# First expert of a routed two-layer kernel: when its weights are split, when the next choice begins, and how far ahead a count is placed

## The chip, the core and the metric

One core of a Trainium2 chip runs the whole kernel. The metric is the time on the device in microseconds, the median of three runs. TensorE (PE) multiplies, VectorE (DVE), ScalarE (ACT) and GpSimd (POOL) work element by element, and SyncE (SP) only issues transfers. Each engine carries out its own list of instructions in the order in which it was written; ACT and POOL issue transfers too, from the same list.

## The reference

Three stages follow one another. Attention with a causal mask and a bias gives x (2304 tokens of 512). Then a routed layer, then a dense one, each token by itself:

```python
logits = x @ w_gate                      # 8 experts, cap = 2304 // 8 = 288
for idx in np.argsort(-flat):            # greedy: best (token, expert) pairs first
    if assigned[tok] >= 0 or counts[e] >= cap: continue
    assigned[tok] = e; counts[e] += 1
out[mask] = np.maximum(x[mask] @ w1[e], 0.0) @ w2[e]     # w1 512x1024, w2 1024x512
...
h = x @ w_in                             # 512 x 2048
g = h * np.tanh(log1p(exp(h)))
return g @ w_out                         # 2048 x 512
```

## The kernel before, in words

All products keep float32 accuracy: each operand is split into a high part, rounded, and a low part, the rest, and a product is three matrix instructions (`mm3`, lines 447 to 449: high by high, high by low, low by high).

After attention, `experts` (line 181 on) fills the experts one after the other, the first one that is full first. `route(e)` finds on the chip which expert is filled next and with which 288 tokens. It takes the best logit of each token, then searches for the largest number of tokens by six counts: two of 64 bins, four of 32. Each count (`search`, line 252) writes a table of comparisons on DVE (`mask`, line 255), counts with 18 small matrix instructions (line 259, result in `rt`), makes `flags` on DVE (line 261), sums them with one more matrix instruction (line 263), and reads the result on DVE (line 267). Then it picks the expert (`ei`, line 315), numbers the tokens, gets their row numbers `idx` (lines 355 and 371) and has POOL gather the rows from memory, three transfers `xg` (line 376). `route` is a generator: each `yield n` says how many places (calls of `step`) of other work are written before its next piece. For the first expert there is no other work, and `route(0)` runs by itself in the loop at line 631. For the others it is written between the matrix products of the expert ahead; it begins at the place `side["next"]` (line 645: 48 places into the first expert, 4 into the later ones). Each group of twelve matrix instructions holds four places.

`up(e)` computes relu(x @ w1) @ w2 for the 288 tokens in eight blocks m of 128 hidden columns. Block m is one group of twelve instructions into a bank `hp` or `words`; ACT makes the high part of the activation (line 508) and DVE the low part (line 509); one group later the twelve instructions of the second layer follow for the block before, into `y`. Each group takes one piece of weights. Such a piece is loaded by SP (`raw`, line 408, 256 KB, four buffers), split by ACT (line 416, high part) and POOL (line 417, low part) into `wt`, which has four buffers. `feed` (line 420) writes loads and splits as buffers allow; `use` (line 431) calls it before a group takes its piece. At the end ACT and DVE turn `y` into `xu` (lines 526 and 527), and `down(e)` runs the dense layer with sixteen blocks f.

The dense layer's weights arrive as 64-bit words. `Convert` (line 32) turns them into floats once, early and beside the first expert: a transfer `r` issued by ACT (line 75, up to 512 KB, three buffers), three pieces on DVE (lines 112, 115, 118), a split by ACT (line 88) and POOL (line 89) into `WI` and `WO`. One call of `conv` writes one piece of DVE; three calls make a unit. `tick` writes one such call, four times for each block m of `up`. Since ACT holds its list while a transfer waits for its buffer, the order of lines 75, 88, 416 and 508 on ACT sets what waits for what. The last piece ahead of the first expert is `conv(5)` (line 640); then 50 idle products keep TensorE busy (`awake`, line 629), and `make_xt` transposes the gathered rows with 20 idle products after each of the three.

Of the kernel before, what the change touches and what calls it, by code (L numbers as in the profile page):

```python
# [28 lines left out]
def fb(ap):  # L29
    return ap.bitcast(F32)  # L30
# [169 lines left out]
def experts(ctx, tc, K, ring, ident, L, x_dram, w1, w2, cv, out):  # L200
# [22 lines left out]
    R = {}  # L223
# [9 lines left out]
    def hbank():  # L233
        if cv.done == 4 * NF2 and len(free) == 2:
            free.insert(0, words)
        free.append(free.pop(0))
        return free[-1]

    def inbank(name):
        at, n = place[name]  # L240
        return bank[:, at:at + n]


    def small(shape, dt, name, bufs=2):
        return rot.tile(shape, dt, name=name, bufs=bufs)

    def route(e):
# [5 lines left out]
        def search(T, lead):  # L253
            mask = small([128, NT, 64], F32R, "mask", 1)
            nc.vector.tensor_tensor(mask[:, :, :T], v[:, :, None].to_broadcast([128, NT, T]),  # L255
                                    jj[:, None, :T].to_broadcast([128, NT, T]), op=OP.is_ge)
            yield lead
            for c in range(NT):
                nc.tensor.matmul(bank[:E, :T], oh[:, c, :], mask[:, c, :T], start=c == 0, stop=c == NT - 1)  # L259
            yield 2  # L260
            nc.vector.tensor_scalar(flags[:E, :T], bank[:E, :T], CAP - 0.5, None, op0=OP.is_ge)
            yield 3
            nc.tensor.matmul(bank[:, 64:64 + T], onesF, flags[:, :T], start=True, stop=True)
            yield 2
            fl = small([128, 64], BF16, "fl", 1)
            J = small([128, 1], F32, "J")
            nc.vector.tensor_scalar(fl[:, 1:T], bank[:, 65:64 + T], 0.5, None, op0=OP.is_ge, op1=OP.add,
                                    accum_out=J)
            R["J"] = J

        if e == E - 1:
            ge = v
            nc.vector.tensor_scalar(ge, m, NEG / 16, None, op0=OP.is_ge)
        else:
            sign = small([128, NT], I32, "sign", 1)
            nc.vector.tensor_scalar(sign, m.bitcast(I32), 31, 0x7FFFFFFF, op0=OP.arith_shift_right,
                                    op1=OP.bitwise_and)
            key, low, high = inbank("sr").bitcast(I32), inbank("low"), inbank("high")
            nc.vector.tensor_tensor(key, m.bitcast(I32), sign, op=OP.bitwise_xor)
            nc.vector.tensor_scalar(high.bitcast(I32), key, 20, 0x4B000800, op0=OP.logical_shift_right,  # L280
                                    op1=OP.bitwise_xor)
            nc.vector.tensor_scalar(v, high, -float(2 ** 23), 2.0 ** -6, op0=OP.add, op1=OP.mult)
            first = search(64, 8)
            n = next(first)
            nc.vector.tensor_scalar(low.bitcast(I32), key, 0xFFFFF, 0x4B000000, op0=OP.bitwise_and,
                                    op1=OP.bitwise_or)
            lf = small([128, NT], F32, "lf", 1)
            nc.vector.tensor_scalar(lf, low, -float(2 ** 23), 2.0 ** -15, op0=OP.add, op1=OP.mult)
            yield n
            yield from first  # L290
            nc.vector.tensor_scalar(v, v, R["J"], 64.0, op0=OP.subtract, op1=OP.mult)
            yield from search(64, 8)
            nc.vector.tensor_scalar(v, v, R["J"], -1.0, op0=OP.subtract, op1=OP.max)
            nc.vector.tensor_scalar(v, v, 1.0, 32.0, op0=OP.min, op1=OP.mult)
            nc.vector.tensor_tensor(v, v, lf, op=OP.add)
            for i in range(4):
                yield from search(32, 6)
                nc.vector.tensor_scalar(v, v, R["J"], 32.0 if i < 3 else 1.0, op0=OP.subtract, op1=OP.mult)
            ge = m
            nc.vector.tensor_scalar(ge, v, 0.0, None, op0=OP.is_ge)  # L300
# [13 lines left out]
        ei = small([1, 1], I32, "ei")  # L314
# [36 lines left out]
        at = bank if e else spare  # L351
# [14 lines left out]
        idx = small([128, NJ], I32, "idx", 3)  # L366
# [26 lines left out]
    raw, wt = {}, {}  # L393
    at = {"load": 0, "split": 0, "use": 0}
    NRAW, NWT = 4, 4

    def load():
        e, m, k = seq[at["load"]]
        at["load"] += 1
        if m == 0 and k == 1:  # L400
            R[e, "reg"] = nc.sync.value_load(R[e, "ei"][0:1, 0:1], min_val=0, max_val=E - 1)
        ev = R[e, "reg"]
        t = rot.tile([128, NC, 128], F32, name="raw", bufs=NRAW)
        if k == 1:
            src = w1[ds(ev, 1), :, 128 * m:128 * m + 128].rearrange("o (c p) f -> p (o c) f", p=128)
        else:
            src = w2[ds(ev, 1), 128 * m:128 * m + 128, :].rearrange("o p (c f) -> p (o c) f", c=NC)
        nc.sync.dma_start(out=t, in_=src)
        raw[e, m, k] = t

    def split():
        key = seq[at["split"]]
        at["split"] += 1
        r = raw.pop(key)
        t = rot.tile([128, 2, NC, 128], F32R, name="wt", bufs=NWT)
        nc.scalar.activation(t[:, 0], r, AF.Copy)  # L416
        nc.gpsimd.tensor_sub(t[:, 1], r, fb(t)[:, 0])  # L417
        wt[key] = t

    def feed(most=99):  # L420
        while True:
            n = at["load"]
            if n < len(seq) and n < at["split"] + NRAW and (seq[n][0], "ei") in R:
                load()
            elif most and at["split"] < min(at["use"] + NWT, at["load"]):
                split()
                most -= 1
            else:
                return

    def use(key):
        assert seq[at["use"]] == key
        feed()
        at["use"] += 1
        return wt.pop(key)

    def conv(n):
        for _ in range(n):
            next(cv.steps, None)
# [13 lines left out]
    side = {"route": None, "at": 0, "next": 0, "conv": (1, 1)}  # L453
# [4 lines left out]
    def tick():  # L458
        now[0] += 1
        for fn, args in todo.pop(now[0], []):  # L460
            fn(*args)
        conv(side["conv"][now[0] % 2])
# [26 lines left out]
    def hl(t):  # L489
        return t[:, 0], t[:, 1]  # L490
# [3 lines left out]
    def up(e):  # L494
        xt = XT.pop(e)
        y, hs = [], {}
        for m in range(NF1 + 1):
            if m < NF1:
                t1 = use((e, m, 1))
                p = hbank()  # L500
                for c in range(NC):
                    mm3(p[:, :CAP], (t1[:, 0, c], t1[:, 1, c]), (xt[:, 0, c], xt[:, 1, c]), c == 0, c == NC - 1)
                    if c < NC - 1:
                        step()
                    if c == 1:
                        tick()
                h = ring("act", [128, 2, CAP], F32R)
                nc.scalar.activation(h[:, 0], p[:, :CAP], AF.Relu)  # L508
                nc.vector.scalar_tensor_tensor(h[:, 1], p[:, :CAP], 0.0, fb(h)[:, 0], op0=OP.max, op1=OP.subtract)
                hs[m] = h  # L510
                tick()
                step()
            if m == 1:
                y = [ps_y.tile([128, 512], F32, name="y") for _ in range(NC)]
            if m > 0:
                t2, h = use((e, m - 1, 2)), hs.pop(m - 1)
                for c in range(NC):
                    mm3(y[c][:, :CAP], (t2[:, 0, c], t2[:, 1, c]), hl(h), m == 1, m == NF1)
                    step()
                    if c == 1 and m < NF1:  # L520
                        tick()
                if m < NF1:
                    tick()
        x2 = ring("xu", [128, 2, NC, CAP], F32R)
        for c in range(NC):
            nc.scalar.activation(x2[:, 0, c], y[c][:, :CAP], AF.Copy)
            nc.vector.tensor_sub(x2[:, 1, c], y[c][:, :CAP], fb(x2)[:, 0, c])  # L527
        X2[e] = x2
        tick()
# [101 lines left out]
    for i, _ in enumerate(route(0)):  # L631
        conv(BUB[i] if i < len(BUB) else 0)
        cv.settle(3)
        if (0, "ei") in R and at["load"] < NRAW:
            feed(0)
        if (0, "ei") in R and (0, "idx") in R and at["split"] < 1:
            feed(1)
    cv.settle(99)
    conv(5)
    awake(50)  # L640
    make_xt(0, range(NJ), 20)
    feed()
    for e in range(E):
        if e + 1 < E:
            side["route"], side["next"] = route(e + 1), side["at"] + (4 if e else 48)
        up(e)
        side["conv"] = (1, 0)
        down(e)
# [486 lines left out]
```

## Time and profile before

| | us |
|---|---|
| median of three runs (1044.93 to 1047.95) | 1045.04 |
| the profiled execution's own time | 1046.98 |
| its span, first to last instruction | 1044.8 |
| TensorE busy in the span | 958.7 (92%) |
| DVE, ACT, POOL busy | 636.2, 624.2, 428.2 |

The profiled execution took 1046.98 us, 2.2 us more than its span and 1.9 us more than the median. From about 335 us on, TensorE is the busiest engine throughout; up to there attention and the first choice run. The profile gives TensorE's granted clock as a share of 2.4 GHz: 1.00 or 0.50.

### The profile page before, as it was taken

What the parts mean: (1) busy time and instruction counts of PE and PEld (TensorE: products, weight loads), DVE (VectorE), ACT (ScalarE), POOL (GpSimd) and SP (SyncE); (2) the same over time, 40 slices, a digit from 0 to 9 for tenths busy, and PEclk for the clock granted to TensorE, in tenths of its full rate; (3) what the DMA queues carried; (4) which work ended last, traced back from release to release, by engine and by line L of the source; (5) the groups of instructions that cost most, each with busy time, mean ns of one, the idle gap of its engine ahead of it and who ended that gap; (6) DMA issues with size and microseconds to landing.
All of it is one profiled execution on the core that took longest, in us unless ns stands there. A gap on an engine that the chain in (4) does not pass through costs nothing.

```text
span 1044.8 us, 21446 instructions
## 1 busy us (share of the span) xinstructions
PE 958.7 (92%) x7695; PEld 924.8 (89%) x7695; DVE 636.2 (61%) x1893; ACT 624.2 (60%) x1389; POOL 428.2 (41%) x424
## 2 busy tenths in 40 slices
PE   6899989999937769899999999999999999999996
PEld 5799888988836669899999999999999999999996
DVE  7667788798676578645654644644655564443243
ACT  4657766676842446645755663673674575675574
POOL 4546666467766722451233126036035123602401
PEclk7869999899967989899999999999999999999998
DMA  5798989895235732330321213123122022500200
GB/s 114 174 198 201 207 186 209 197 209 133 64 104 156 213 98 82 104 104 2 89 74 47 64 51 95 41 63 106 29 77 86 20 79 71 152 12 29 77 2 23
DMA packets 133298, 105.57 MB, mean 101 GB/s; under 512 B 63720, under 2 KB 114056, under 8 KB 133160
## 3 DMA queue, kind: packets, MB, share of 16 engines
q1 hardware_dynamic: 122520, 83.50, 32.7%
q10 hardware_dynamic: 7600, 11.27, 3.5%
q0 software_dynamic: 3072, 9.44, 2.9%
q8 instruction: 60, 0.98, 0.4%
q14 instruction: 46, 0.38, 0.1%
HBM read 69.55 MB, written 9.73 MB: 76 GB/s over the span
## 4 chain that ended last, share of the span: by engine, by line
PE 47%; issue 6%; DVE 3%; POOL 1%; ACT 1%; DMA 1%; POOLq 0%; ACTq 0%
PE y L447 8%; PE y L448 7%; PE y L449 7%; PE hp L447 5%; PE hp L449 4%; PE hp L448 4%; PE words L447 3%; PE words L449 3%; PE words L448 2%; PE rt L259 2%; DVE mask L255 1%; PE hp L481 0%; PE rt L355 0%; PE hp L608 0%; POOL wt L417 0%
## 5 line engine op out<-in xcount | busy, mean ns | idle before, releaser
L417 POOL TENSOR_TENSOR wt<-raw,wt 128x512 fp32r<-128x512 f32 x128 | 163.3, 1291 | 177.0 <-ACT wt L416 168.5
L953 POOL TENSOR_TENSOR Pl<-P,Ph 128x384 fp32r<-128x384 f32 (+2 forms) x128 | 136.6, 1074 | 96.6 <-DVE Ph L952 44.4
L447 PE MATMUL y<-act,WO 128*128 128x288 f32 x512 | 155.3, 303 | 0.0
L448 PE MATMUL y<-act,WO 128*128 128x288 f32 x512 | 152.3, 297 | 0.2
L449 PE MATMUL y<-act,WO 128*128 128x288 f32 x512 | 152.3, 297 | 0.0
L447 PE MATMUL hp<-xu,WI 128*128 128x288 f32 x368 | 111.7, 304 | 7.2 <-DVE c L547 5.4
L416 ACT ACTIVATE wt<-raw 128x512 fp32r<-128x512 f32 x128 | 79.8, 625 | 51.8 <-DMA raw<-in_moe_w_dram 16.1
L449 PE MATMUL hp<-xu,WI 128*128 128x288 f32 x368 | 109.1, 296 | 0.0
L448 PE MATMUL hp<-xu,WI 128*128 128x288 f32 x368 | 107.8, 293 | 0.8 <-DVE xu L527 0.8
L376 POOL DMA_INDIRECT xg<-x_dram,idx x24 | 22.5, 938 | 184.9 <-DVE rt L382 179.7
L448 PEld LDWEIGHTS y<-act,WO 128*128 128x128 f32 x512 | 97.4, 190 | 0.6 <-DVE act L553 0.6
L449 PEld LDWEIGHTS y<-act,WO 128*128 128x128 f32 x512 | 97.8, 191 | 0.0
L447 PEld LDWEIGHTS y<-act,WO 128*128 128x128 f32 x512 | 97.6, 191 | 0.0
L945 ACT ACTIVATE P<-s 128x384 f32<-128x384 f32 (+2 forms) x128 | 63.8, 503 | 41.1 <-PE s L938 24.2
L539 ACT ACTIVATE c<-c 128x288 f32<-128x288 f32 x128 | 56.5, 441 | 43.0 <-DVE c L538 39.0
L447 PE MATMUL y<-act,wt 128*128 128x288 f32 x256 | 79.5, 310 | 1.6 <-ACT act L508 1.6
L547 DVE SCALAR_TENSOR_TENSOR hp<-c,hp 128x288 f32<-128x288 f32 x75 | 34.6, 461 | 75.2 <-ACT c L542 75.1
L973 PE MATMUL pv<-Ph,VH 128*128 128x320 f32 (+4 forms) x224 | 74.3, 332 | 4.8 <-DVE xT L992 4.5
L447 PEld LDWEIGHTS hp<-xu,WI 128*128 128x128 f32 x368 | 69.3, 188 | 10.1 <-DVE c L547 6.9
L448 PE MATMUL y<-act,wt 128*128 128x288 f32 x256 | 76.7, 300 | 0.2
L449 PE MATMUL y<-act,wt 128*128 128x288 f32 x256 | 76.3, 298 | 0.2 <-POOL wt L417 0.2
L936 PE MATMUL s<-QKB 128*128 128x320 f32 (+4 forms) x224 | 72.3, 323 | 0.8 <-DVE mx L874 0.8
(253 smaller groups left out, 2956.8 us busy)
## 6 DMA issues: line engine op xcount, KB each, us to landing
raw<-in_moe_w_dram SPq DMA_DIRECT2D x128, 256.0 KB
QKB<-qk SPq DMA_DIRECT2D x55, 288.0 KB
QKA<-qk SPq DMA_DIRECT2D x29, 288.0 KB
qkraw<-in_q_dram SPq DMA_DIRECT2D x32, 128.0 KB
qkraw<-in_k_dram SPq DMA_DIRECT2D x32, 128.0 KB
vraw<-in_v_dram SPq DMA_DIRECT2D x32, 128.0 KB
x_dram<-xn SPq DMA_DIRECT2D x16, 256.0 KB
r<-in_moe_w_in_dram ACTq DMA_DIRECT2D x8, 512.0 KB
```

The source lines that it names most:

```text
L376: nc.gpsimd.indirect_dma_start(out=xg[:JW], out_offset=None, in_=x_dram, in_offset=bass.IndirectOffsetOnAxis(ap=idx[:JW, j:j + 1], axis=0))
L416: nc.scalar.activation(t[:, 0], r, AF.Copy)
L417: nc.gpsimd.tensor_sub(t[:, 1], r, fb(t)[:, 0])
L447: nc.tensor.matmul(out_ap, ah, bh, start=first, stop=False)
L448: nc.tensor.matmul(out_ap, ah, bl, start=False, stop=False)
L449: nc.tensor.matmul(out_ap, al, bh, start=False, stop=last)
L539: nc.scalar.activation(a, a, AF.Exp)
L547: nc.vector.scalar_tensor_tensor(u, a, 0.5, p[:, :CAP], op0=OP.subtract, op1=OP.mult)
L936: nc.tensor.matmul(p[:m, at:at + n], KB[i][:, h, kc], QB[i][:, h, q0:q1], start=ti in (1, 2) and j == 0, stop=False, skip_group_check=True)
L945: nc.scalar.activation(P[:, :n], p[:, :n], AF.Exp, scale=0.125)
L953: nc.gpsimd.tensor_sub(Pl[:, :n], P[:, :n], fb(Ph)[:, :n])
L973: nc.tensor.matmul(o, VH[i][:, a, hs], ph, start=first, stop=False)
```

## The change

Five edits. The first count of a choice is placed 14 places after its table instead of 8, in every choice but the last. `use` calls `feed` only if its piece isn't split yet; `up` calls `feed` after each block's activation and after each group of the second layer. In the loop of `route(0)` the loads go out as soon as the expert is known, and from its 30th yield one piece is split at each yield until three are. Nine calls of `conv` instead of five stand ahead of the first transposes. The second choice begins 24 places into the first expert instead of 48.

```diff
-            first = search(64, 8)
+            first = search(64, 14)
...
     def use(key):
         assert seq[at["use"]] == key
-        feed()
+        if key not in wt:
+            feed()
...
                 hs[m] = h
+                feed()
                 tick()
                 step()
...
                     if c == 1 and m < NF1:
                         tick()
+                feed()
                 if m < NF1:
                     tick()
...
         cv.settle(3)
-        if (0, "ei") in R and at["load"] < NRAW:
-            feed(0)
-        if (0, "ei") in R and (0, "idx") in R and at["split"] < 1:
-            feed(1)
+        if (0, "ei") in R:
+            feed(0 if i < 29 or at["split"] > 2 else 1)
     cv.settle(99)
-    conv(5)
+    conv(9)
...
         if e + 1 < E:
-            side["route"], side["next"] = route(e + 1), side["at"] + (4 if e else 48)
+            side["route"], side["next"] = route(e + 1), side["at"] + (4 if e else 24)
```

How the instructions move, at three places. In the rows a number after a name tells buffers apart; behind line 433 the changed kernel's line numbers are one to three higher. First POOL where the first expert's rows are gathered, before:

```order
L89 TENSOR_TENSOR WO_4553<-c_4853,WO_4553 128x256
L376 DMA xg<-x_dram,idx 96x512 x3
L417 TENSOR_TENSOR wt<-raw,wt 128x512
L89 TENSOR_TENSOR WI_4554<-c_4931,WI_4554 128x256
L89 TENSOR_TENSOR WI_4554<-c_4960,WI_4554 128x256
```

and now:

```order
L89 TENSOR_TENSOR WO_4553<-c_4818,WO_4553 128x256
L417 TENSOR_TENSOR wt<-raw,wt 128x512 x3
L89 TENSOR_TENSOR WO_4553<-c_4853,WO_4553 128x256
L376 DMA xg<-x_dram,idx 96x512 x3
L89 TENSOR_TENSOR WI_4554<-c_4946,WI_4554 128x256
```

Three splits and nothing else have come ahead of the conversion that stood before the gathers; four splits that stood behind them are now two.

Second, ACT from the activation of block 2 of the first expert to that of block 3, before (`WI8` and `WO8` are the weights of one block f of the dense layer, `WI9` of the next):

```order
L508 ACTIVATE act_5202<-hp1_4586 128x288
L416 ACTIVATE wt_5206<-raw_5108 128x512
L88 ACTIVATE WI8_4556<-r2_5116 128x512
L75 DMA r2_5226<-in_moe2_w_out_dram 128x512
L416 ACTIVATE wt_5229<-raw_5133 128x512
L508 ACTIVATE act_5247<-hp0_4585 128x288
```

and now:

```order
L509 ACTIVATE act_5210<-hp1_4586 128x288
L416 ACTIVATE wt_5213<-raw_5120 128x512
L88 ACTIVATE WO8_4557<-r2_4984 128x512
L75 DMA r2_5227<-in_moe2_w_in_dram 128x4x128
L416 ACTIVATE wt_5236<-raw_5141 128x512
L88 ACTIVATE WI9_4558<-r2_5152 128x512
L509 ACTIVATE act_5257<-hp0_4585 128x288
```

The two splits stand between the same two activations as before; the conversions are those that stood one block later.

Third, DVE from the end of the second choice (line 386 writes the used tokens out of the logits; the gathers are issued just before it) to the transposed rows of the second expert, before:

```order
L386 TENSOR_TENSOR L<-L,rt 128x144
L547 SCALAR_TENSOR_TENSOR hp_4586<-c_6267,hp_4586 128x288
L553 SCALAR_TENSOR_TENSOR act<-hp_4586,act 128x288
L485 TENSOR_TENSOR xu<-words,xu 128x4x96
```

and now:

```order
L386 TENSOR_TENSOR L<-L,rt 128x144
L541 TENSOR_SCALAR c_6209<-hp_4586 128x288
L556 SCALAR_TENSOR_TENSOR act<-hp_4585,act 128x288
L550 SCALAR_TENSOR_TENSOR hp_4586<-c_6209,hp_4586 128x288
L541 TENSOR_SCALAR c_6248<-words 128x288
L556 SCALAR_TENSOR_TENSOR act<-hp_4586,act 128x288
L550 SCALAR_TENSOR_TENSOR words<-c_6248,words 128x288
L556 SCALAR_TENSOR_TENSOR act<-words,act 128x288
L541 TENSOR_SCALAR c_6283<-hp_4585 128x288
L550 SCALAR_TENSOR_TENSOR hp_4585<-c_6283,hp_4585 128x288
L556 SCALAR_TENSOR_TENSOR act<-hp_4585,act 128x288
L486 TENSOR_TENSOR xu<-hp_4586,xu 128x4x96
```

Three blocks of the dense layer now stand between the end of the choice and the transposes. On PE, between line 355 and the first transpose, there are 72 matrix instructions in place of 18. The DVE block that opens the second choice (lines 249 to 288) stands behind the activation of block 3 of the first expert, before behind that of block 6, and the second count of 64 has come from the dense layer into `up`, its table behind the activation of block 5. In `up` the count's flags (line 261) stand on DVE behind the activation of block 5, and PE's sum of them inside the second layer's group for block 4.

## Rows read from the trace of the kernel before

**Rows 1.** The page's head.
```profile
span 1044.8 us, 21446 instructions
```

**Rows 2.** Windows: stretch, length; busy (count) of PE, PEld, DVE, ACT, POOL; clock; DMA.
```profile
319.68:323.60 3.92, 0.92 (x8) 0.72 (x7) 3.33 (x14) 0.00 (x0) 0.00 (x0) 0.50 0.69 202
...
334.33:376.61 42.28, 30.85 (x215) 28.20 (x213) 25.90 (x53) 16.77 (x35) 29.66 (x25) 0.92 0.64 192
...
438.97:445.10 6.13, 6.13 (x28) 6.11 (x29) 1.11 (x2) 0.98 (x2) 0.14 (x1) 0.50 0.17 51
...
369.87:373.42 3.55, 3.55 (x29) 3.55 (x30) 2.38 (x5) 0.97 (x2) 0.81 (x2) 0.50 0.52 146
445.10:530.76 85.66, 84.69 (x737) 83.97 (x736) 46.28 (x139) 50.57 (x114) 26.05 (x25) 1.00 0.22 64
```

**Rows 3.** Waits of PE from 334 us on: waiter, releaser, total, times, longest.
```profile
PE rt L259 <- DVE lf L288: 8.1, 6, 5.8
PE hp L447 <- DVE c L547: 5.4, 7, 1.7
PE words L481 <- DMA xg<-x_dram,idx: 3.4, 1, 3.4
```

**Rows 4.** Waits of PE from 446 us on, experts two to eight: all there are.
```profile
PE hp L447 <- DVE c L547: 2.5, 5, 0.5
PE rt L259 <- DVE lf L288: 2.4, 5, 0.5
```

**Rows 5.** Timeline of ACT, first expert: activations of blocks 2 to 7, a transfer, xu.
```profile
341.48 0.39 ACT L508 ACTIVATE act<-hp 128x288 fp32r<-128x288 f32 x1
...
347.25 0.34 ACTq L75 DMA_DIRECT2D r<-in_moe_w_out_dram  x1
...
348.22 0.39 ACT L508 ACTIVATE act<-hp 128x288 fp32r<-128x288 f32 x1
...
353.40 0.39 ACT L508 ACTIVATE act<-hp 128x288 fp32r<-128x288 f32 x1
...
359.83 0.41 ACT L508 ACTIVATE act<-hp 128x288 fp32r<-128x288 f32 x1 [2.05 <-PE hp L449]
...
365.22 0.39 ACT L508 ACTIVATE act<-hp 128x288 fp32r<-128x288 f32 x1
...
372.54 0.40 ACT L508 ACTIVATE act<-hp 128x288 fp32r<-128x288 f32 x1
...
376.15 1.30 ACT L526 ACTIVATE xu<-y 128x288 fp32r<-128x288 f32 x4
```

**Rows 6.** Timeline of SP: the first expert's loads.
```profile
319.68 38.79 SPq L408 DMA_DIRECT2D raw<-in_moe_w_dram  x16
```

**Rows 7.** Timeline of POOL: conversion ahead of the gathers, first gather, first split.
```profile
325.07 0.74 POOL L89 TENSOR_TENSOR WO<-c,WO 128x256 fp32r<-128x256 f32 x1 [7.42 <-ACT WO L88]
325.99 1.13 POOL L376 DMA_INDIRECT xg<-x_dram,idx  x1 [0.17 <-DVE rt L384]
...
329.59 1.29 POOL L417 TENSOR_TENSOR wt<-raw,wt 128x512 fp32r<-128x512 f32 x1
```

**Rows 8.** Timeline of PE: start, length, instruction, count, [idle before, releaser].
```profile
324.77 5.06 PE L629 MATMUL y<-onesF,upperF 128*64 128x128 f32 x50
...
369.87 1.13 PE L259 MATMUL rt<-mask,oh 128*8 128x64 f32 x18 [5.77 <-DVE lf L288]
...
432.12 0.93 PE L355 MATMUL rt<-aux,mask 128*96 128x6 bf16 x18
```

**Rows 9.** Timeline of DVE: first and last of the opening block; the next table.
```profile
366.61 0.30 DVE L249 TENSOR_REDUCE rt<-L 128x18 f32<-128x144 f32 x1
...
369.64 0.18 DVE L288 TENSOR_SCALAR lf<-rt 128x18 f32<-128x18 f32 x1
...
376.01 1.36 DVE L255 TENSOR_TENSOR mask<-rt,jj 128x1152 fp32r<-128x1152 f32 x1
```

**Rows 10.** The chain of waits at the first expert's end: the gather.
```profile
435.74 3.10 DMA xg<-x_dram,idx
```

## The prediction, made before the changed kernel ran

> **What bounds the kernel now.** The head and the windows [rows 1, 2] come first. In the second expert PE works 84.69 of 85.66 us: from there on little but PE's own work is left. The 576 products of such an expert take at most 84.69 / 576 = 0.147 us each (its few counts and transposes are in that), so a group of twelve takes 1.7 us and a block of `up`, two groups, 3.5 us. The first expert's `up` is another matter: 42.28 us, of which PE works 30.85, POOL 29.66, DVE 25.90, ACT 16.77. No engine is full, so they wait for each other.
>
> The waits of PE [rows 3, 4] say where. One first count waited 5.8 us, in the first expert; the first transposes of the second expert's rows waited 3.4; the five later experts that search have two waits of 0.5 us each, 2.4 and 2.5 us together, and nothing else.
>
> What sets the pace of the first `up` is seen on ACT [rows 5]. The activations of blocks 2 to 7 start 6.74, 5.18, 6.43, 5.39 and 7.32 us apart, and xu follows 3.61 us after the last. PE would need 3.5. Between two activations ACT's list holds splits, conversions and a transfer, such as that at 347.25, less than a microsecond ahead of the next activation; the transfer holds the list until POOL has read the buffer that it fills, POOL needs ACT's conversion, that needs DVE's third piece, and DVE's pieces stand behind the low part of the activation. This ring goes round once for each unit of the dense layer's weights, 1.33 units to a block, and PE only looks on. What shortens PE's part or POOL's alone gains nothing there.
>
> **The change, part by part.** *Three splits ahead of the gathers.* The loads go out at 319.68 [rows 6]; by 323.60 202 GB/s times 3.92 us, 792 kB, have moved, the three pieces of 262 kB [rows 2]. POOL has been idle 7.42 us until 325.07 and gathers at 325.99 [rows 7]. Now three splits of 1.29 us come first, 3.9 us. Behind a split that waits stand that conversion and the gathers, and behind these all of the first expert. The first can't start before the first piece is in (about 322) and ACT's half is done (0.6): 322.6. They end at 326.5 at the soonest, 327.3 if each piece is noticed a little late, then the conversion of 0.74 follows that ended at 325.81. So the gathers start 1.4 to 2.2 us later; I take 1.9. What hides it: the 50 idle products, which end at 329.83 [rows 8]. A gather takes 3.10 us [rows 10], so the first rows land about 329.1 and at most 0.7 us of cover is left. I take 1.6 us for the start of `up`, 335.9 in place of 334.33 [rows 2], and 0.7 to 2.2 as its bounds. The three splits moved away from behind the gathers saved nothing there: PE didn't wait for them.
>
> *Splits behind the activation.* In ACT's rows the same two splits stand between the same two activations as before; only the order against conversions changes. Cost and gain nothing; if a split were late, it would be PE's 0.5 to 1.4 us waits of the old `up`, which lie inside the ring's time.
>
> *Four pieces more converted ahead.* They run on DVE while the gathers are under way, at no cost. But the list is now 1.33 units ahead of PE's blocks: what stood between activations 3 and 4 now stands between 2 and 3. So the ring does the same number of turns per block, plus one before xu, and starts earlier by what the buffers allow. I count with the old intervals by content, from the activation of block 1. PE ends block 1 two groups after 335.9, at 339.4. Then: one unit, 5.4 (the shorter of the two plain intervals with one unit); two units, 5.2; one unit and the block that opens the second choice, 369.82 - 366.61 = 3.2 [rows 9], 8.6; one unit, 5.4; two units, 7.32 - 3.21 = 4.1, and the table of the second count, 1.36, with half a microsecond around it, 6.0; one unit, 5.4; one unit before xu, 3.6. Sum 39.6: xu at 379.0 in place of 376.15, **+2.9 us**. If every one-unit turn took 3.6 us, it would be 7.2 less; if each took the mean of the three, 6.2, 3.2 more. Bounds -4.3 and +6.1.
>
> *The second choice begins 24 places sooner.* In `up` its opening block now delays block 4 and not block 7; that is in the sum. Inside `up` PE also waits for the first count's flags: they stand on DVE behind the activation of block 5, which waits for the ring, while PE has only block 4's second-layer group ahead. I expect some 5 us of PE waiting there, as long as the old 5.77 [rows 8]; the ring doesn't wait for PE, so it is not added. The dense layer loses one count of 64: 1.13 us at half clock, so **-0.6**. At the end of the first expert the gathers come 72 products before the transposes instead of 18. Line 355 ended at 433.05 [rows 8], and the rows were there at 438.84 [rows 10], 5.8 us; 72 products at full clock take 9.6 to 10.6. So the wait of 3.42 goes [rows 3], and with it the 6.13 us at 1.2 GHz that followed [rows 2], half of which, 3.07, was lost: **-6.5**. What is late next there: nothing within 3.8 us.
>
> *Clock at the start of the dense layer.* PE will have waited several microseconds before xu. After the old waits of 5.77 and 3.42 us, and only after those, the clock stood at 0.50, for 3.55 and 6.13 us of PE's work [rows 2]. The first dense groups wait for DVE and ACT anyway (1.7 us at most, [rows 3]). I take **+1.0**, bounds 0 and +3.1.
>
> *Six more places ahead of a first count.* Six places are 18 products, 2.4 us; the wait was 0.5. It goes in five experts: -2.4 [rows 4]. The counts behind it move by as much against the dense layer's blocks; the wait for `c` of 0.5 us has a table of a count ahead of it on DVE, which now comes earlier or later. I take half of 2.5: **-3.6** together, bounds 0 and -4.9.
>
> Sum: 2.9 - 0.6 - 6.5 + 1.0 - 3.6 = -6.8 us. The profiled execution's 1046.98, with its span of 1044.8, becomes 1040.2; against the median of 1045.04 that is **1038.2 us**. All low ends together give -16.3, all high ones +3.1; the sum of them all on one side is unlikely.
>
> **The rivals.** *POOL paces the first `up`.* If four pieces ahead free the ring, POOL's queue is left: behind the gathers (3.6 us from 327.9) 13 splits and 11 conversions up to the last split, 24 times 1.3 = 31 us, so 362.7, the last group 1.7: xu at about 364.5, 11.7 us sooner instead of 2.9 later, and no cold start. 1038.2 - 14.6 - 1.0 = 1022.6. For it: POOL worked 29.66 of 42.28 us. Against it: the same contents between activations as before.
>
> *The clock falls before `up`.* Between the idle products' end and the first transposes PE now idles some 1.6 us. In the old `up` waits that short did no harm: its mean clock of 0.92 [rows 2] is 3.4 us lost in 42.28, no more than the one stretch around the 5.77 us wait. If it falls, `up` starts at 1.2 GHz, and the ring's first activations, which still wait for PE, are late by up to half of 6.13 us: 1038.2 + 3.1 = 1041.3. The Trainium skill (TensorE: Matmul & The Clock Gate, Part 1) says that the gate halves the clock when PE has been too little busy, and that only sustained work brings it back. By that rule the broken cover of idle products speaks against this edit; the two rows at 0.50 agree with it, and no row shows a lull of this size and kind.
>
> *The gather is not relieved.* POOL's queue ahead of it holds three splits of the next expert, which wait for their loads; if they are late the transposes still wait 3.4 us and lose the clock: 1038.2 + 6.5 = 1044.7, no change. Against it: the next expert is known 18 places sooner too.
>
> *Slower: the clock stays down.* If PE's waits for flags, activations and xu follow so closely that it never works long enough, the clock stays at 1.2 GHz from block 4 to the fourth dense group. Then four dense groups take 1.7 us more each and two of `up` in the ring as well, 10.2 in all: 1038.2 + 10.2 = 1048.4. It decides when PE idles again for some 3 us before each stretch of work. Against it: the old mean of 0.92 says that after the 5.77 us wait the clock came back within the same stage.
>
> **How the numbers follow.** About 0.3% (3.1 us) is what a measurement of this kernel tells from no change. Chances: the sum 0.60, POOL pace 0.10, early fall of the clock 0.14, gather not relieved 0.09, clock down 0.07. The range 1029 to 1045 leaves out POOL pace and the slow clock, 0.17. Faster by over 0.3% (below 1041.9): 0.51 of the sum's 0.60, half of the early fall, POOL pace: 0.68; within: 0.24; slower: 0.08.
>
> **What would show it.** After: xu of the first expert at 377 to 383 and activations 5 to 9 us apart; a wait of PE for the first count's flags of several microseconds inside `up`; first gather on POOL at 327.4 to 328.2; no wait of transposes for `xg` and no 0.50 clock at the first expert's end; no wait at line 259 in the later experts. Wrong would be: activations under 5 us apart throughout (POOL pace), or waits for `xg` that stay.

## The result and the profile after

The changed kernel takes **1056.51 us** (1055.07 to 1058.93) where the kernel before, run beside it, takes 1044.99: 1.0108 times as long, with a 95% interval of 1.0079 to 1.0136. Forecast were 1038.2 and a range up to 1045. It is slower, by about 1%, and none of the rivals gave that time.

The profiled execution took 1055.66 us. First its head and its windows by stage, with columns as in [rows 2]: the first load to the first product of `up`, the first `up`, the first xu to the second, the second xu to the third.

```profile
span 1053.7 us, 21450 instructions
```

```profile
320.93:342.00 21.07, 13.49 (x143) 12.90 (x142) 11.42 (x37) 5.43 (x11) 9.47 (x10) 0.64 0.69 192
335.24:342.00 6.76, 6.76 (x73) 6.60 (x73) 1.59 (x4) 1.98 (x4) 0.00 (x0) 0.68 0.49 128
342.00:385.30 43.30, 32.04 (x233) 29.55 (x231) 29.13 (x60) 15.98 (x32) 28.78 (x23) 0.88 0.55 164
385.30:482.60 97.30, 90.03 (x765) 87.19 (x766) 59.59 (x166) 55.45 (x121) 35.34 (x32) 0.96 0.28 84
482.60:568.70 86.10, 85.00 (x738) 83.92 (x737) 47.38 (x140) 50.83 (x114) 26.24 (x25) 1.00 0.22 64
```

And the same stages in the trace of the kernel before.

```profile
319.68:334.33 14.65, 11.63 (x143) 11.35 (x142) 9.70 (x33) 3.85 (x9) 6.36 (x7) 0.68 0.55 167
334.33:376.15 41.82, 30.84 (x214) 28.19 (x212) 25.44 (x53) 16.31 (x33) 29.38 (x24) 0.92 0.64 190
376.15:477.00 100.85, 91.23 (x785) 88.25 (x786) 65.49 (x182) 55.94 (x124) 37.76 (x34) 0.97 0.30 88
477.00:562.60 85.60, 84.63 (x737) 83.91 (x736) 46.91 (x140) 50.54 (x114) 26.09 (x25) 1.00 0.23 64
```

The span grew by 8.9 us, and the rows say where. The first load goes out 1.25 us later (320.93 for 319.68). Nothing is changed ahead of it, and in the runs below it comes anywhere from 318.24 to 321.57 us, so that is attention's own scatter, and the reason why stages are compared here and not spans alone. Then: to the first product of `up` **+6.4** us, the first `up` **+1.5**, from xu to xu **-3.5** (the windows above are cut at rounded times), and from the second xu to the end 571.1 us (1053.7 - 482.6) for 567.8, **+3.3**. Sum 8.9. Forecast were +1.6, +1.3, -6.1 and, for the later counts, -3.6.

Where the 6.4 us arise is seen on SP, ACT, POOL and PE (timelines, in this order): loads and transfers, the gathers, the transposes of the gathered rows.

```profile
325.85 2.82 SPq L408 DMA_DIRECT2D raw<-in_moe_w_dram  x3
...
328.75 0.35 ACTq L75 DMA_DIRECT2D r<-in_moe_w_out_dram  x1
...
330.20 0.39 ACTq L75 DMA_DIRECT2D r<-in_moe_w_in_dram  x1
...
331.66 0.34 ACTq L75 DMA_DIRECT2D r<-in_moe_w_out_dram  x1
...
329.17 1.13 POOL L376 DMA_INDIRECT xg<-x_dram,idx  x1 [0.18 <-issue]
...
331.82 0.92 POOL L376 DMA_INDIRECT xg<-x_dram,idx  x1 [0.30 <-issue]
...
335.24 0.90 PE L482 MATMUL hp<-ident,xg 96*128 96x96 f32 x4 [4.56 <-DMA xg<-x_dram,idx]
...
340.44 0.52 PE L482 MATMUL hp<-ident,xg 96*128 96x96 f32 x4
```

The first gather goes out 8.24 us behind the first load, 6.31 before [rows 6, 7]: 1.93 later. But its rows are there 6.07 us after that, not 3.1 [rows 10]. The three gathers of the changed kernel land 6.0, 7.6 and 8.3 us after their issue. The table of DMA issues (last number: median us from issue to landing, of the transfers whose landing it could tell) has the gathers of the changed kernel and then those of before:

```profile
xg<-x_dram,idx POOLq DMA_INDIRECT x3, 7.6
```

```profile
xg<-x_dram,idx POOLq DMA_INDIRECT x3, 3.3
```

Three loads of weights (0.79 MB), sent at 325.85 into the buffers that the early splits had emptied, and three transfers for the dense layer (1.3 MB), two of them (1.05 MB) sent by the four pieces more that are converted, are under way at the same time. PE waits 4.56 us, and then its clock is at 0.50 for the first transposes, as the first of these windows shows:

```profile
335.24:339.60 4.36, 4.36 (x35) 4.20 (x36) 0.56 (x1) 0.91 (x2) 0.00 (x0) 0.50 0.74 195
387.41:390.80 3.39, 3.39 (x23) 3.39 (x20) 1.71 (x4) 1.61 (x4) 1.30 (x1) 0.50 0.09 31
428.88:431.76 2.88, 2.88 (x12) 2.88 (x13) 0.98 (x2) 1.08 (x2) 1.81 (x2) 0.50 0.27 91
```

The other two rows stand in the first dense layer. The waits of PE there, and below the dots all that it has in one later expert (482.6 to 568.7):

```profile
PE words L448 <- DVE r L118: 2.8, 1, 2.8
PE hp L448 <- ACT xu L529: 2.5, 1, 2.5
PE hp L448 <- DVE c L550: 2.0, 2, 1.5
...
PE words L448 <- DVE act L510: 0.4, 1, 0.4
PE rt L263 <- DVE flags L261: 0.4, 1, 0.4
PE rt L259 <- DVE mask L255: 0.3, 1, 0.3
```

The wait for `xg` of [rows 3] is gone, as forecast; one of 2.8 us for the last conversion's third piece has come, which holds the bank `words`. In a later expert the two waits of [rows 4] are gone and three others stand there.

### The profile page after: what moved, and what is told of

It is laid out like the page before. It is cut to its first block, busy times and chain, and to the rows that moved or that the text cites. A ratio compares the mean times of both kernels' runs of the same rounds, so it can differ in the third digit from the quotient of the medians.

```text
span 1053.7 us, 21450 instructions
## 1 busy us (share of the span) xinstructions
PE 958.2 (91%) x7695; PEld 921.8 (87%) x7695; DVE 639.3 (61%) x1893; ACT 626.2 (59%) x1389; POOL 428.9 (41%) x424
## 4 chain that ended last, share of the span: by engine, by line
PE 43%; DVE 8%; issue 7%; ACT 5%; POOL 1%; ACTq 0%; POOLq 0%
PE y L448 7%; PE y L449 7%; PE y L450 7%; PE hp L448 4%; PE hp L450 4%; PE hp L449 4%; PE words L448 3%; PE words L450 2%; PE words L449 2%; DVE mask L255 2%; PE rt L259 1%; ACT c L543 1%; ACT c L544 1%; ACT c L545 1%; ACT c L542 1%
## 5 line engine op out<-in xcount | busy, mean ns | idle before, releaser
L448 PEld LDWEIGHTS hp<-xu,WI 128*128 128x128 f32 x364 | 69.2, 190 | 7.7 <-ACT xu L529 4.1
L449 PEld LDWEIGHTS hp<-xu,WI 128*128 128x128 f32 x364 | 69.6, 191 | 0.6 <-DVE xu L530 0.6
```

What stands on the lines that cost most here:

```text
L448: nc.tensor.matmul(out_ap, ah, bh, start=first, stop=False)
L449: nc.tensor.matmul(out_ap, ah, bl, start=False, stop=False)
```

## The experiments

Stages of every profiled execution, in us, worked out from the starts of SP's first load, PE's first product of `up` and the xu instructions on ACT, and from the span: first load to first product, first `up`, first xu to second, third expert, sixth expert (to the seventh xu), first load to the end. The kernel before, repeated beside the runs, has medians of 1045.45 to 1046.13 in the sets timed in several rounds. Its single times there run from 1041.97 to 1055.05, so the rows marked (one), timed once, go by their stages.

Not every stage repeats equally well where no edit touches it. `up` does: 43.25 to 43.33 in four kernels that differ only ahead of it. The stage to `up` lies between 14.50 and 15.39 in before, a_lead14, a_start24 and b_feed_start, which have the same program up to there: PE doesn't wait for rows in them, and its 50 idle products take from 4.76 to 5.57 us, as the clock rises earlier or later in or behind them. With the change it is 20.67 to 21.07 (after, u_noload, u_lead8, u_oldfeed). From xu to xu u_conv5 and u_order_only, alike from `up` on, are 1.4 us apart. Differences below these belong to no edit.

| run | time | to `up` | `up` | xu to xu | third | sixth | load to end |
|---|---|---|---|---|---|---|---|
| before | 1044.99 | 14.65 | 41.82 | 100.81 | 85.65 | 83.55 | 725.1 |
| after | 1056.51 | 21.07 | 43.30 | 97.36 | 86.1 | 85.2 | 732.8 |
| u_noload | 1054.77 | 21.07 | 43.33 | 97.35 | 86.1 | 85.2 | 732.9 |
| u_conv5 | 1049.45 | 18.63 | 40.20 | 96.68 | 86.1 | 85.2 | 726.7 |
| u_oldsplit | 1051.97 | 16.51 | 43.67 | 97.14 | 86.2 | 85.2 | 728.9 |
| u_hold | 1050.56 (one) | 18.14 | 43.25 | 96.15 | 86.1 | 85.2 | 728.6 |
| u_order_only | 1046.30 (one) | 16.17 | 40.19 | 98.09 | 86.1 | 85.2 | 725.6 |
| u_awake120 | 1055.33 (one) | 20.51 | 43.31 | 97.14 | 86.1 | 85.2 | 732.3 |
| u_lead8 | 1051.24 | 20.67 | 42.88 | 96.66 | 85.65 | 85.2 | 729.5 |
| a_lead14 | 1052.37 | 14.50 | 41.46 | 105.00 | 86.2 | 84.1 | 731.4 |
| u_oldfeed | 1056.28 (one) | 20.77 | 44.88 | 98.25 | 86.1 | 84.1 | 733.9 |
| a_start24 | 1045.39 | 15.39 | 41.30 | 98.11 | 85.65 | 84.0 | 723.2 |
| b_feed_start | 1042.07 | 15.25 | 39.25 | 98.80 | 85.65 | 83.6 | 721.3 |
| b_conv2 | 1040.66 | 14.45 | 38.28 | 98.63 | 85.65 | 83.6 | 719.3 |

### What makes the gathers late

**u_noload**, the changed kernel with

```diff
-            feed(0 if i < 29 or at["split"] > 2 else 1)
+            if i < 29:
+                feed(0)
+            elif at["split"] < 3:
+                split()
```

> The changed kernel, but the three early splits fetch no new weights: the loads of pieces 5 to 7 go out only behind the transposes of the gathered rows. Theory (transfers): the three gathers land 6.0, 7.6 and 8.3 us after their issue, not 3.3, because 0.79 MB of loads and 1.3 MB of the dense layer's words share the DMA engines with them; without the loads, at some 300 GB/s, the last rows land about 2.6 us sooner, up starts about 2.6 us sooner and the clock falls for a shorter stretch: 1052 to 1054. Rival (the queue of POOL): the gathers are late because three splits stand ahead of them, and their landing time is not changed by the loads: still 6 to 8 us, 1056 to 1057.

Nothing moved: 21.07 us, as with the whole change. The trace shows why: SP sent the first of the three loads 5.0 us behind the very first (323.23 - 318.24), 4.9 in the changed kernel. They stand later in the program, but SP has nothing to do ahead of them, and a free buffer is all that they wait for. The run tells nothing of the loads.

**u_conv5**: `conv(9)` is `conv(5)` again in the changed kernel.

> The changed kernel with five conversions ahead of the first transposes again, not nine. Theory (transfers): two transfers of 512 KB for the dense layer leave the time of the gathers; the last rows land about 3.4 us sooner, up starts that much sooner; the first up itself loses the pieces that were ahead and holds one more turn of the ring, +1 to +3 us there: 1053 to 1056. Rival (the queue of POOL): the gathers still take 6 to 8 us and up starts no sooner: 1056 to 1059.

`up` begins 2.4 us sooner, and the first `up` is not longer but 3.1 us shorter. 1.0037 times the kernel before (1.0020 to 1.0053). The transposes still wait, and 0.50 follows for one stretch:

```profile
331.26 0.90 PE L482 MATMUL hp<-ident,xg 96*128 96x96 f32 x4 [2.69 <-DMA xg<-x_dram,idx]
```

Here the low clock costs time: from the first transposes to the first product PE works 6.03 us without a wait, for 4.69 in u_order_only below, at 1.00.

```profile
331.26:337.29 6.03, 6.03 (x73) 6.03 (x73) 1.60 (x4) 1.99 (x4) 0.75 (x2) 0.75 0.13 35
```

**u_oldsplit**: the old `if` with `feed(0)` and the one split is back in the loop.

> The changed kernel with the old loop ahead of the first expert: loads as buffers allow up to four, one split behind the row numbers. Theory (transfers): no loads of pieces 5 to 7 beside the gathers, and POOL reaches the first gather some 2 us sooner; the rows land after 4 to 5 us, only the dense layer's words are beside them; the clock stays up; up starts 4 to 6 us sooner: 1050 to 1052.5. Rival (the words of the dense layer alone slow the gathers): the gathers still take 6 us or more, and only the 2 us are won: 1054 to 1055.

`up` begins at 16.51 us, 4.6 sooner, 1.9 behind the kernel before: with conversions ahead alone, the third gather is the late one (a wait of 1.37 us at the third transposes). Time 1.0066 times that of before (1.0043 to 1.0089).

**u_hold**: the loads really held, on top of u_noload, by

```diff
     make_xt(0, range(NJ), 20)
+    nc.sync.value_load(R[0, "xg"][NJ - 1][0:1, 0:1].bitcast(I32))
     feed()
```

> The changed kernel, with the loads of pieces 5 to 7 made to wait on SyncE until the last gather has landed (in the earlier attempt they were only written later, and SyncE sent them at once, since a buffer was free). Theory (loads and words share the engines): the gathers land after 4.5 to 6 us in place of 6.0 to 8.3, and up starts 1 to 2.5 us sooner than 21.15 us behind the first load. Rival (the words of the dense layer alone): the gathers still take 6 to 8 us and up starts at most 0.5 us sooner.

18.14 us: 2.9 sooner, so the loads share the blame. PE waits 2.20 us for the first rows:

```profile
331.90 0.90 PE L482 MATMUL hp<-ident,xg 96*128 96x96 f32 x4 [2.20 <-DMA xg<-x_dram,idx]
```

**u_order_only**: u_hold with `conv(5)`. Only the three splits ahead of the gathers are left.

> The changed kernel with both companions of the gathers taken away: five conversions ahead of the transposes, and the loads of pieces 5 to 7 held on SyncE until the last gather has landed. What stays is the order of POOL's queue, three splits ahead of the gathers, which the prediction priced at 1.6 us. Theory (the order costs what was predicted, the transfers the rest): the first gather goes out 8.3 us behind the first load, two later than before; the gathers land after 3.1 to 3.5 us each; up starts 16 to 16.6 us behind the first load, 14.65 before and 21.07 with the whole change; clock 1.00 there. Rival (the order alone breaks the cover and the clock falls): up starts at 17.5 us or later, with a stretch at 0.50 between the transposes and the first products.

16.17 us, 1.5 behind the kernel before, and no 0.50 in or behind the transposes. First gather and first transposes:

```profile
327.15 1.13 POOL L376 DMA_INDIRECT xg<-x_dram,idx  x1 [0.17 <-issue]
...
330.51 0.55 PE L482 MATMUL hp<-ident,xg 96*128 96x96 f32 x4 [1.33 <-DMA xg<-x_dram,idx]
```

The kernels add up. The order of POOL's queue costs 1.5 us (u_order_only against before, give or take the scatter of 0.9 us in that stage of before). The words of the dense layer cost 1.9 (u_oldsplit against before), 2.0 (u_hold against u_order_only) or 2.4 (after against u_conv5), the loads 2.5 (u_conv5 against u_order_only) or 2.9 (after against u_hold). Together 5.9 to 6.8, and the whole is 6.4. The 2.5 of u_conv5 are 1.1 for later first rows (12.6 us behind the first load, 11.5 in u_order_only) and 1.3 for the low clock.

**u_awake120**: `awake(50)` is `awake(120)` in the changed kernel.

> The changed kernel with 120 idle products instead of 50 ahead of the first transposes, so that PE is busy until about a microsecond before the late rows land. Theory (the late rows cost twice, by the wait and by the clock): no stretch at 0.50 between the idle products and up; from the first transposes to the first product of up 4.7 us as before, not 6.76; up starts 19 us behind the first load, 2 sooner. Rival (the clock costs nothing here): 21 us all the same.

The clock stayed up, and yet `up` began only 0.56 us sooner. Window from the first transposes to the first product:

```profile
335.88:341.88 6.00, 5.02 (x76) 4.76 (x74) 1.59 (x4) 1.99 (x4) 0.00 (x0) 1.00 0.50 132
```

My 2 us were wrong: at full clock the second and third transposes wait for their own rows (0.63 and 0.35 us). The landing of the last rows sets the start, and the low clock ran beside that. Even 0.56 is an upper bound: u_lead8 and u_oldfeed, which change nothing ahead of `up`, begin it 0.4 and 0.3 us sooner than the changed kernel too.

### What lengthens the later experts

**u_lead8**: `search(64, 14)` is `search(64, 8)` again in the changed kernel.

> The changed kernel with the first count 8 places behind its table again, not 14. Theory (lead): the longer later experts (86.1 us from one xu to the next, 85.65 before) come from the counts' new places, which put two waits for flags and a table where one wait stood and lay bare a wait for the low part of an activation; with 8 they are 85.65 again and the last searching expert 83.5: about 3 us less, 1053 to 1054.5. Rival (splits behind the activation): the later experts are longer because of where the splits are written; then they stay at 86.1 and gain the old wait of 0.5 us back: 1056.5 to 1059.

1051.24 us, 1.0051 times before (1.0033 to 1.0069): 5.3 less than the changed kernel by the medians, 3.3 by the stages from the load on. The third to fifth experts take 85.65 us again, with two waits as in [rows 4]; the sixth stays at 85.2, so the lead alone doesn't explain it.

**a_lead14**: the kernel before with `search(64, 14)` alone.

> The kernel before with one edit: the first count stands 14 places behind its table, not 8. Theory (lead): the waits at the first count go, but waits for flags, a table and a low part of an activation come, and the later experts take 86.1 us instead of 85.65, the sixth 83.5 as before; the first expert's wait of 5.8 us for the first count moves but stays: 1046 to 1048. The prediction's sum: later experts 0.5 to 1 us shorter each, 1041.5 to 1043.

1052.37 us, 1.0061 times before (1.0044 to 1.0079). More than either theory: the later experts do take 86.2, and the second choice, started at its old place, ends later, so that PE waits 7.3 us for the rows of the second expert, 3.4 before [rows 3]:

```profile
PE words L481 <- DMA xg<-x_dram,idx: 7.3, 1, 7.3
```

**u_oldfeed**: the three edits of `use` and `up` undone in the changed kernel.

> The changed kernel with splits written where they were before: feed in every use, none behind the activation or the second layer's group. Theory: the sixth expert, 85.17 us to the next xu with the change also where the lead is 8 again, and 83.55 before, is longer because a split stands on ACT ahead of xu (PE waited 1.07 us for xu there); with the old places it is 83.5 again and that wait is gone; the other later experts stay at 86.1 (lead); the first up stays within 0.5 us of 43.3. Rival: the sixth expert is longer because of when its choice begins or the lead; then it stays at 85.2.

The sixth expert takes 84.1, not the 83.5 expected, and the wait for xu there is gone, as expected. But the first `up` is 1.6 us longer: the splits' new places gain 1.6 us there (the 0.9 more from xu to xu is inside that stage's scatter) and lose 1.1 in the sixth. The row of the changed kernel (timeline of ACT) shows the split that is written ahead of the sixth expert's xu:

```profile
911.68 0.63 ACT L416 ACTIVATE wt<-raw 128x512 fp32r<-128x512 f32 x1 [0.95 <-PE y L450]
912.22 1.29 ACT L529 ACTIVATE xu<-y 128x288 fp32r<-128x288 f32 x4
```

### What gains

**a_start24**: the kernel before with 24 in place of 48.

> The kernel before with one edit: the second choice begins 24 places into the first expert, not 48. Theory (the gain is this edit alone): no wait for the gathered rows of the second expert and no fall of the clock there, as in all kernels with the edit, where the dense layer of the first expert took 67.4 us to the next product of up, not 71.5; up starts as before, 14.7 us behind the first load, and takes 40 to 42 us; later experts 85.65 as before: 1039 to 1041. Rival (the gain needs the other edits, or the waits for flags in the first up take it back): 1044 to 1046.

1045.39 us, 0.9981 times before (0.9961 to 1.0001): between the two theories. From load to end it is 1.9 us shorter. xu to xu loses 2.7 us, not 4: the wait for the gathered rows is gone, but PE waits 2.9 us for low parts of activations, 1.0 before, and 1.5 for `words`, 0.5 before.

**b_feed_start**: the kernel before with the early choice and the new places of the splits, the last of them left out (the edits of `use` and behind the activation as in the change).

```diff
                         tick()
                 if m < NF1:
+                    feed()
                     tick()
...
-            side["route"], side["next"] = route(e + 1), side["at"] + (4 if e else 48)
+            side["route"], side["next"] = route(e + 1), side["at"] + (4 if e else 24)
```

> The kernel before with two of the five edits: the second choice begins 24 places in, and the splits are written behind the activation and behind the second layer's groups (but not behind the last of them, where a split would stand on ACT ahead of xu). Lead 8, five conversions and the old loop stay. Theory (stage by stage, from the runs so far): first product of up 14.7 us behind the first load, up 40 to 41, the first dense layer 67 to 68, then 29.3, 85.65 four times, 83.5 to 84.1, 79.2 and 62.5 to the end: 718.5 to 721 us from the first load to the end, 4 to 6.5 less than before: 1039 to 1042. Rival (the split places gain only where other edits have made room): 723, as with the early choice alone, 1043 to 1045.

1042.07 us, 0.9968 times before (0.9944 to 0.9992); 721.3 from load to end, both just above what the theory gave. `up` takes 39.25, the sixth expert 83.6.

**b_conv2**: the same with `conv(2)` in place of `conv(5)`.

> As the kernel with two edits, but with two conversions ahead of the first transposes instead of five. Theory (ring): nine instead of five cost 3.1 us in the first up, one turn of the ring more; two, one unit less, save one turn: up 36.5 to 38.5 us, and the dense layer of the first expert still has its weights in time: 2 to 3.5 us less than with five. Rival (the ring's turns are owed anyway): what up gains is lost in the dense layer, where PE waits for a conversion; within 1 us of five.

1040.66 us, **0.9946 times before** (0.9923 to 0.9969), the lowest median here, though its interval overlaps that of b_feed_start:

```profile
span 1040.3 us, 21447 instructions
```

`up` takes 38.28, 1.0 less than with five, and the dense layer does not give it back. From load to end it is 1.9 less, just under the 2 to 3.5 expected, but 0.8 of that lies ahead of `up`, inside that stage's scatter. So fewer pieces ahead make `up` shorter here, 3.1 us for four and 1.0 for three; a turn of the ring is not simply won with three.

## Why the prediction was wrong, point by point

**Start of `up`, forecast +1.6, measured +6.4: the step that failed.** The order was priced well: first gather 1.93 us later for 1.9, order alone 1.5 for 1.6 (0.8 to 1.7 with the scatter of that stage). The gather's own 3.10 us was the wrong part. It was read from [rows 10], the end of the first expert, and used for a place where the same change sends 1.8 MB more to the same DMA engines. Of the splits I counted POOL's time, but not what a split does to its buffer: it empties it, and SP fills it at once. Of the four conversions I wrote "at no cost", and each unit of them sends a transfer. Both are DMAs of moved steps.

**The first `up`, forecast 43.1 us (335.9 to 379.0), measured 43.30.** The ring paces it, as forecast, but that the number came so close is in part luck. The activations of blocks 2 to 7 and xu in the trace after:

```profile
350.44 0.41 ACT L509 ACTIVATE act<-hp 128x288 fp32r<-128x288 f32 x1 [1.28 <-PE y L450]
...
355.69 0.39 ACT L509 ACTIVATE act<-hp 128x288 fp32r<-128x288 f32 x1
...
364.22 0.41 ACT L509 ACTIVATE act<-hp 128x288 fp32r<-128x288 f32 x1 [1.83 <-POOL WO L89]
...
369.02 0.41 ACT L509 ACTIVATE act<-hp 128x288 fp32r<-128x288 f32 x1 [1.27 <-POOL WI L89]
...
374.98 0.40 ACT L509 ACTIVATE act<-hp 128x288 fp32r<-128x288 f32 x1
...
380.52 0.41 ACT L509 ACTIVATE act<-hp 128x288 fp32r<-128x288 f32 x1 [1.84 <-POOL WO L89]
...
385.29 1.32 ACT L529 ACTIVATE xu<-y 128x288 fp32r<-128x288 f32 x4 [1.78 <-POOL WI L89]
```

The intervals are 5.25, 8.53, 4.80, 5.96, 5.54 and 4.77 us; forecast were 5.2, 8.6, 5.4, 6.0, 5.4 and 3.6. ACT waits for POOL's conversions ahead of four of them, which is the ring. PE only looks on: its wait for the first count's flags came too, 3.2 us for the 5 forecast.

```profile
PE rt L263 <- DVE flags L261: 3.2, 1, 3.2
```

u_conv5 and u_order_only confirm the cause: without the four pieces `up` takes 40.2. But then they cost 3.1 us, more than the +1.3 forecast, and the splits' new places, priced at nothing, gave 1.6 back (u_oldfeed: 44.88). The two errors have opposite signs.

**Splits behind the activation, forecast 0:** 1.6 us gained in the first `up`, 1.1 lost in the sixth expert (u_oldfeed). The order between the activations in the first `up` was all I compared; the last `feed` of `up`, ahead of xu, was not looked at.

**xu to xu, forecast -6.1 (-0.6, -6.5, +1.0), measured -3.5.** The wait of 3.42 us and its stretch at 1.2 GHz went. In their place came 2.8 us for `words` and 12 products that took 2.88 us at 0.50. "What is late next there: nothing within 3.8 us" was asked of the transposes alone. The end of the choice, moved forward, now stands on DVE between two pieces of the last conversion, which holds the bank that PE needs next. The start of the dense layer cost 1.7 (3.39 us at 0.50) for +1.0, inside its bounds. PE's busy time fell by 1.2 us (91.23 to 90.03, the moved count in it) and its idle time by 2.35, but the time that it worked at 0.50 did not fall at all: 6.13 us before, 3.39 and 2.88 after. The low clock was moved, not won back. The small waits that also changed were not taken apart.

**Later counts, forecast -3.6, measured +3.3: the second step that failed, in its sign.** Not all of the 3.3 is the lead's. The four experts at 86.1 make 1.8 and the sixth 1.6, of which 1.1 is the split ahead of its xu; where its other 0.5 comes from stays open, since a_start24, with the old lead and the old splits, has 84.0 too. PE's wait for the first count's opening block did go. The three that came, 1.1 us together, are no smaller than the two that went, 1.0; and PE's busy time for the same work rose from 84.63 to 85.00, for which no run shows the reason. The bound 0 at the upper end had no reason: each count of the chain moves against DVE's other work, and I had priced only the one that was late. One of the three stands where the removed wait stood, 62.7 us behind xu (545.26) for 62.2 before (539.17): a product into `words` waits until DVE, making an activation's low part, has read that bank, and DVE gets to it behind the opening block, which runs from 541.63 to 544.84. So DVE is late there whoever asks first, and the edit bared that wait; no run took it apart further.

**The rivals.** The gathers were relieved; POOL did not pace `up`. The clock did fall ahead of `up`, as one rival had it, but u_awake120 puts that at 0.56 us at most, not 3.1 (with the loads alone beside the gathers, in u_conv5, it cost 1.3). It did not stay down: it was 0.50 from 363.5 to 373.7 us and back at 1.00 before `up` ended. Of the rivals, the one that lost the most, 1048.4, still lay 8 us below the result, since each had kept the gather at 3.1 us and the later counts at a gain. The sum of the high ends is wrong too: 6.1 - 0.6 - 6.5 + 3.1 gives +2.1, not +3.1.

## What to carry to other kernels

A step that empties a buffer, or takes one more piece off a list, also sends what refills it: before it is moved ahead of a transfer that something waits for, the bytes it sets loose must be added to that transfer's time. Where a short wait at one place in a chain of dependent steps is removed by moving its start, price every later step of the chain against what now stands beside it, and ask what was hidden behind the wait. Splitting a bundle of edits paid: two of the five, one of them in part, with one number turned the other way, beat both kernels.

## What had not been expected of the hardware

Three gathers of 0.59 MB together landed 3.1 to 3.3 us after issue when 0.26 MB of other transfers ran beside them (u_order_only), and 6.0 to 8.3 when 2.1 MB of other transfers were under way: the small transfer that everything waited for had no precedence. A load written later in the program went out no later (u_noload). An idle stretch of 1.33 us on PE, ahead of the first transposes, left the clock at 1.00; behind one of 2.20 us it was 0.50. The windows from those transposes on, u_order_only and then u_hold:

```profile
330.51:335.20 4.69, 4.69 (x72) 4.69 (x73) 1.59 (x3) 1.98 (x4) 1.66 (x3) 1.00 0.35 112
```

```profile
331.90:335.20 3.30, 3.30 (x27) 3.30 (x28) 0.56 (x1) 0.49 (x1) 1.85 (x3) 0.50 1.02 322
```

The length of such a gap does not decide it alone. In b_conv2 a wait of 2.41 us inside `up` left the clock at 1.00 for the 15 us that followed, and one of 1.45 us in the dense layer was followed within a microsecond by 0.50:

```profile
350.88 0.73 PE L259 MATMUL rt<-mask,oh 128*8 128x64 f32 x18 [2.41 <-DVE lf L288]
...
390.49 0.29 PE L259 MATMUL rt<-mask,oh 128*8 128x32 f32 x5 [1.45 <-DVE mask L255]
```

```profile
350.88:365.90 15.02, 9.95 (x97) 9.25 (x97) 11.06 (x22) 6.58 (x13) 11.09 (x10) 1.00 0.58 167
391.30:394.70 3.40, 3.40 (x17) 3.40 (x16) 2.20 (x6) 1.84 (x5) 1.30 (x1) 0.50 0.16 28
```
